# A state-space block with its FFN on one core: the first transposing load moves to ScalarE's queue, two evictions move to VectorE, and the written-out order changes

## The chip, the core and the metric

The kernel runs on one core of a Trainium2 chip. That core has a matrix engine (TensorE, PE in the profile; its weight loads are PEld), three engines for element-wise work (VectorE or DVE, ScalarE or ACT, GpSimd or POOL), and SyncE (SP), which here only issues DMAs. TensorE writes its results to PSUM, from where ScalarE or VectorE must copy ("evict") them to SBUF. DMAs are issued on the queue of an engine, SyncE's or ScalarE's, and the transfers of both are carried out by the core's 16 DMA engines. The metric is the device time of one execution in microseconds, as the median of several runs; lower is better.

## The reference

Inputs: q, k, v and the output are 2048 x 640 in bf16 (sequence by channels). Cut to what matters:

```python
k_shift = sum over t of 4 taps: k delayed by t * shift_k[:, t]     # short causal filter per channel
kv = k_shift * v
y  = causal convolution of kv with ssm_k along the sequence (by FFT in the reference) + kv * ssm_D
h  = x + layernorm(x) * y                                          # x is q
h2 = h + (silu(layernorm(h) @ w_gate) * (layernorm(h) @ w_up)) @ w_down
```

w_gate and w_up are 640 x 1728, w_down is 1728 x 640.

## The kernel before, in words

The sequence is cut into four blocks (0 to 3) of 512. The long convolution is done by blocks: each block of kv and each of the four blocks of the filter ssm_k is turned into a 512-point spectrum by matmuls with cosine and sine tables (`ftab`), spectra are multiplied and added on VectorE, and matmuls with `itab` turn them back.

The work of the front, before the first FFN, is:
- **Filter blocks 0 to 3.** `kload` (L527) loads block m of ssm_k into the tile kc; `ktrans` (L530) transposes it on TensorE in two groups of ten 128x128 transposes (L538), and ScalarE evicts each group to KT (L543). `kfwd` turns KT into spectra by `halves` (L573): matmuls L582, eviction L595 into C, R1 and KO, then butterflies on VectorE (L552). For block 0, VectorE also adds ssm_D to one row of KT (L547, "D", task 34) before the matmuls of kf0 may start.
- **kv.** `kv` (L671) loads k of the block transposed (channels on partitions) into kT with a transposing DMA (`tload`, L481, issued at L484) and v into vt. TensorE applies the four taps in three matmul groups (L691 for channels 0 to 511, L686 for the rest); ScalarE evicts them (block 0: L698; others: L715). In block 0 TensorE transposes the result back (L706) and VectorE multiplies it with v (L711); in the others transposing DMAs (kvo<-kT) do that and VectorE multiplies at L724. kT shares its memory with IO, an input of the inverse transform, so k of block i+1 can be loaded only when TensorE has read IO of block i.
- **The spectrum of kv** (`xfwd`: L582, evicted at L595 into X and FO), products (L753 to L769), the **inverse** (`inverse`, L817: matmuls L830, evicted at L845 by VectorE in block 0 and at L854 by ScalarE in blocks 1 to 3), the second layernorm, and a transposing DMA of the result into hnT (hnT<-qo). The FFN (L911, L912, L922, then the down-projection L954, L966) follows on hnT.

TensorE starts with 24 matmuls on zeros (L511, "spin"), which compute nothing. ScalarE's first ACTIVATE is a dummy Silu (L516), with the load of the function table in front of it.

**What sets the order.** Every operation is a numbered task, in the order in which the code adds them. `ORDER` (L307) is a table written out by hand or by a search outside of the kernel: for each of the five engines' queues the numbers of its tasks in the order in which they are issued. `schedule` walks it to assign PSUM tiles (four of two banks each), and `emit` puts semaphore waits in front of each task and writes the queues. A queue is worked off in its order: a task that waits holds back all behind it. The costs in the code serve that walk alone (PSUM tiles, and where `schedule` puts filler matmuls, L249, into a gap of TensorE that it foresees).

Task numbers that matter here: 0 identity matrix; 1 and 2 wcol and drow (the taps and ssm_D, on ScalarE's queue); 3 ftab; 13 spin; 14 Silu; 15 and 16 the tap matrices dg and dl on VectorE; 17, 57, 62, 67 the loads of filter blocks 0 to 3; 18 the transposing load of k, block 0; 19 v; 138 x, block 0. 20, 24 and 28 are the matmul groups of kv0, 21, 25 and 29 their evictions. 32 and 35 are the two groups of transposes of filter block 0, 33 and 36 their evictions. 37 to 52 are kf0 (odd: matmuls, even: evictions). 139 to 151 are the bn_stats of x. 192 to 195 are the inverse of block 0; 202, 209, 216, 223 its hnT transposes. 312, 313, 314 are x, k and v of block 1; 315, 319, 323 the matmul groups of kv1, 316, 320, 324 their evictions. 802 to 805 are the inverse of block 3 and 806, 815, 824, 833 its evictions.

Before the change tasks 18, 33 and 806 stand on the queues of SyncE, ScalarE and ScalarE.

Of the kernel before, what the change touches and what calls it, by code (L numbers as in the profile page):

```python
# [23 lines left out]
class _Task:  # L24
    __slots__ = ("eng", "fn", "cost", "lat", "deps", "after", "succ", "npred", "ready", "end", "start",
                 "opens", "tiles", "idx", "clock", "sem", "seq", "dma", "name", "gap", "lock", "fill", "late", "pause")
# [32 lines left out]
class _Graph:  # L59
# [38 lines left out]
    def add(self, eng, name, fn, cost, r=(), w=(), pr=(), pw=(), skip=(), lat=None, dma=None, after=(), lock=None):  # L98
# [9 lines left out]
        t.fill = 0  # L108
        t.pause = None
# [120 lines left out]
    def emit(self, block):  # L230
# [84 lines left out]
    """,  # L315
    "act": """
# [12 lines left out]
    """,  # L329
    "dve": """  # L330
# [10 lines left out]
    """,  # L341
    "pool": """
        5 10 6 8 7 9 11 153 197 218 204 200 211 221 207 214 338 423 405 396 414 531 626 608 599 617 734 838 820 829 811
    """,
    "sp": """
# [3 lines left out]
    """,  # L349
}  # L350


def bass_sequential_preLN__ssm_conv_h3__swiglu_ffn__prompt_kernel(
    nc: bass.Bass,
# [713 lines left out]
```

## Time and profile before

| | |
|---|---|
| median of 3 runs | 273.35 us (273.2 to 273.37) |
| profiled execution: first to last instruction (span) | 269.5 us |
| PE busy | 255.2 us (95%) |
| ScalarE busy | 206.9 us (77%) |
| VectorE busy | 203.8 us (76%) |
| DMA moved | 25.85 MB, 96 GB/s on the mean |
| granted TensorE clock | 0.998 |

The profile is one execution on the chip. Its times count from the first instruction; what lies outside of the span (the program's start and end) isn't in it. L12 is line 12 of the kernel before. A row such as `ACT L543 ACTIVATE KT<-ps 128x1280 x2 | idle` names the engine, the line, the operation, what it writes and reads, and how many of them are taken together; a bracket at the end gives the idle time of the engine before it and what ended it. SPq and ACTq are the queues' own instructions, such as the issuing of a DMA. The chain of waits follows the work that ended last back in time: each step goes to what released it. In the list of stretches each engine has its busy time; a row of DMA issues gives the bytes and the time from issue to landing; the rows "q8 instruction" and "q14 instruction" are the fetches of the engines' own program, in count, MB and share.

### The profile page before, as it was taken

To read this page: it belongs to the slowest core of one execution; us is meant where nothing else is said; L and a number is where in the kernel's file an instruction comes from. 1 tells how busy PE (TensorE), PEld (TensorE's weight loads), DVE (VectorE), ACT (ScalarE), POOL (GpSimd) and SP (SyncE) were. 2 spreads that over 40 slices of the span, in tenths; PEclk is the share of its full clock that TensorE was granted. 3 is DMA by queue.
4 is the path that set the end of the run, shared out by engine and by line. 5 is a ranking of instruction groups with operands and counts; after the bars stand their busy time and mean duration, and the time that the engine had idled before them with its cause. 6 is when DMAs were issued, how large, how long until landed. Compare 5 with 4: busy or idle time off the path is not lost.

```text
span 269.5 us, 4198 instructions
## 1 busy us (share of the span) xinstructions
PE 255.2 (95%) x1643; PEld 144.2 (53%) x1660; DVE 203.8 (76%) x282; ACT 206.9 (77%) x394; POOL 24.1 (9%) x35
## 2 busy tenths in 40 slices
PE   7799797999999999999999997999999999999995
PEld 5576455545444666554446574454446674444663
DVE  2399999899999999999999998999996100042312
ACT  2799999797889999479969997399889963647400
POOL 0000315000030013000200141000200200000000
PEclk9999999999999999999999999999999999999999
DMA  6999909551173608643000336510000050010002
GB/s 124 373 355 369 340 19 124 112 138 73 30 261 122 103 0 103 135 155 100 0 1 16 86 63 119 129 80 1 2 0 0 2 122 0 2 49 0 0 27 99
DMA packets 42501, 25.85 MB, mean 96 GB/s; under 512 B 32241, under 2 KB 41202, under 8 KB 42482
## 3 DMA queue, kind: packets, MB, share of 16 engines
q1 hardware_dynamic: 41824, 25.58, 35.7%
q8 instruction: 13, 0.21, 0.3%
q10 hardware_dynamic: 658, 0.01, 0.1%
q14 instruction: 6, 0.05, 0.1%
HBM read 15.69 MB, written 2.62 MB: 68 GB/s over the span
## 4 chain that ended last, share of the span: by engine, by line
DVE 41%; PE 27%; ACT 19%; DMA 6%; SPq 3%; issue 2%; POOL 1%; DVEq 0%
PE ps L954 11%; DVE T L753 6%; DVE T L754 6%; PE ps L912 6%; PE ps L911 5%; DVE T L759 5%; DVE Y L769 5%; DVE gu L938 4%; DVE X L552 3%; SPq L484 3%; DMA kT<-in_A_k_dram 3%; ACT KT L543 3%; ACT KO L595 2%; DVE C L666 2%; DMA kc<-in_A_ssm_k_dram 2%
## 5 line engine op out<-in xcount | busy, mean ns | idle before, releaser
L954 PE MATMUL ps<-Wd,gu 128*128 128x384 bf16 (+1 forms) x416 | 59.0, 299 | 0.2 <-ACT qo L854 0.2
L912 PE MATMUL ps<-hnT,UA 128*128 128x512 bf16 x140 | 53.1, 379 | 0.5
L911 PE MATMUL ps<-hnT,GA 128*128 128x512 bf16 x132 | 50.0, 379 | 1.3 <-DMA hnT<-qo 1.3
L954 PEld LDWEIGHTS ps<-Wd,gu 128*128 128x128 bf16 x416 | 40.0, 98 | 18.3 <-issue 1.3
L936 ACT ACTIVATE ub<-ps 128x512 bf16<-128x512 f32 (+1 forms) x60 | 33.7, 568 | 18.5 <-PE ps L912 11.3
L912 PE MATMUL ps<-hnT,UB 128*128 128x512 bf16 x120 | 45.5, 379 | 0.2
L911 PE MATMUL ps<-hnT,GB 128*128 128x512 bf16 x117 | 44.3, 379 | 0.0
L938 DVE TENSOR_TENSOR gu<-gu,ub 128x512 bf16<-128x512 bf16 x52 | 21.5, 421 | 25.1 <-ACT ub L936 13.2
L934 ACT ACTIVATE gu<-ps 128x512 bf16<-128x512 f32 x52 | 29.8, 596 | 12.6 <-PE ps L912 12.4
L753 DVE TENSOR_TENSOR T<-X,C 128x2560 bf16<-128x2560 bf16 x20 | 29.7, 1486 | 0.2
L754 DVE TENSOR_TENSOR T<-X,C 128x2560 bf16<-128x2560 bf16 x20 | 29.7, 1486 | 0.1
L911 PEld LDWEIGHTS ps<-hnT,GA 128*128 128x128 bf16 x140 | 13.7, 98 | 18.2 <-DMA hnT<-qo 1.9
L582 PE MATMUL ps<-KT,ftab 128*128 128x320 bf16 x128 | 19.9, 300 | 2.5 <-ACT KT L543 1.8
L912 PEld LDWEIGHTS ps<-hnT,UA 128*128 128x128 bf16 x140 | 13.7, 98 | 15.7
L881 POOL TENSOR_TENSOR mv<-mv,half 128x1 f32<-128x1 f32 x16 | 13.7, 859 | 68.2 <-ACT mv L874 68.2
L911 PEld LDWEIGHTS ps<-hnT,GB 128*128 128x128 bf16 x120 | 11.7, 98 | 14.2 <-ACT ub L936 0.2
L759 DVE TENSOR_TENSOR T<-T 128x1280 bf16<-128x1280 bf16 x24 | 19.2, 819 | 0.1
L912 PEld LDWEIGHTS ps<-hnT,UB 128*128 128x128 bf16 x120 | 11.7, 98 | 14.0
L582 PE MATMUL ps<-vt,ftab 128*128 128x320 bf16 x128 | 19.0, 299 | 0.1
L804 POOL TENSOR_TENSOR st<-st,half 128x8 f32<-128x8 f32 x4 | 7.9, 1981 | 113.1 <-ACT st L798 113.1
L769 DVE TENSOR_TENSOR Y<-Y,T 128x2560 bf16<-128x2560 bf16 x12 | 17.8, 1484 | 0.0
L582 PEld LDWEIGHTS ps<-KT,ftab 128*128 128x128 bf16 x128 | 11.0, 98 | 10.7 <-ACT KT L543 3.1
(86 smaller groups left out, 376.5 us busy)
## 6 DMA issues: line engine op xcount, KB each, us to landing
kc<-in_A_ssm_k_dram SPq DMA_DIRECT2D x4, 640.0 KB, 10.1
vt<-in_A_v_dram SPq DMA_DIRECT2D x4, 640.0 KB, 4.8
xh<-in_A_q_dram SPq DMA_DIRECT2D x4, 640.0 KB, 5.9
out_dram<-xh SPq DMA_DIRECT2D x16, 160.0 KB, 2.0
Wd<-in_B_w_down_dram SPq DMA_DIRECT2D x1, 1280.0 KB, 7.5
UA<-in_B_w_up_dram SPq DMA_DIRECT2D x1, 1120.0 KB, 13.5
GA<-in_B_w_gate_dram SPq DMA_DIRECT2D x1, 1120.0 KB, 10.5
UB<-in_B_w_up_dram SPq DMA_DIRECT2D x1, 960.0 KB, 7.5
```

The lines of the kernel that those rows point to most:

```text
L582: last = e.matmul(pt.f(c, W), ftab[:, cs, j, f * P:(f + 1) * P], src[:, j, c * W:(c + 1) * W], start=(j == par), stop=(j == par + 2))
L753: g.add("dve", nm, lambda e, x=x, k=k, t1=t1: e.tensor_tensor(out=t1, in0=x, in1=k, op=ALU.mult), cdve(2560), r=[x, k], w=[t1])
L754: g.add("dve", nm, lambda e, x=x, k=ksw, t2=t2: e.tensor_tensor(out=t2, in0=x, in1=k, op=ALU.mult), cdve(2560), r=[x, k], w=[t2])
L759: g.add("dve", nm, lambda e, p=p, q=q, d=d, op=op: e.tensor_tensor(out=d, in0=p, in1=q, op=op), cdve(1280), r=[p, q], w=[d])
L769: g.add("dve", nm, lambda e, y=y, z=z: e.tensor_tensor(out=y, in0=y, in1=z, op=ALU.add), cdve(2560), r=[y, z], w=[y])
L881: g.add("pool", nm, lambda e, m=m: e.tensor_tensor(out=m[:, 3:4], in0=m[:, 2:3], in1=half[:, 1, 0:1], op=ALU.pow), 650, r=[m[:, 2:3], half ...
L911: e.matmul(pt.f(0, N), wg[:, c, f0:f0 + P], hnT[:, c, :], start=(c == 0), stop=(c == NC5 - 1))
L912: last = e.matmul(pt.f(1, N), wu[:, c, f0:f0 + P], hnT[:, c, :], start=(c == 0), stop=(c == NC5 - 1))
L934: g.add("act", nm, lambda e, pt=pt, gv=gv, a=ps_g, ts=ts: e.activation(out=gv, in_=pt.f(a[0], N, a[1])[:, ts], func=ACTF.Silu, scale=gain) ...
L936: g.add("act", nm, lambda e, pt=pt, uv=uv, a=ps_u, ts=ts: e.activation(out=uv, in_=pt.f(a[0], N, a[1])[:, ts], func=ACTF.Copy, scale=gain) ...
L938: g.add("dve", nm, lambda e, uv=uv, gv=gv: e.tensor_tensor(out=gv, in0=gv, in1=uv, op=ALU.mult), cdve(n), r=[gv, uv], w=[gv])
L954: last = e.matmul(pt.flat(c1 - c0, P + c0), slots[fb][:, j * P:(j + 1) * P], Wd[:, fb, c0:c1], start=(fb == 0 and not second), stop=(fb == ...
```

## The change

There are three edits.
1. `tload` takes the queue as an argument, and for block 0 the transposing load of k (task 18) is issued on ScalarE's queue.
2. A new helper `evict` makes the PSUM evictions that were written out before. For the numbers in `VECTOR` (33 and 806) it makes them on VectorE as tensor_copy or tensor_scalar; for all others the same ACTIVATE as before.
3. `ORDER` has new lists for all five queues.

The code (the unchanged lines around and the other callers of `evict` are left out):

```diff
+VECTOR = """
+    33 806
+"""
...
+        def evict(name, out, src, n, w, pr, scale=1.0, bias=None, r=(), after=()):
+            if len(g.tasks) in on_vector:
+                if bias is None and scale == 1.0:
+                    fn = lambda e: e.tensor_copy(out=out, in_=src())
+                elif bias is None:
+                    fn = lambda e: e.tensor_scalar(out=out, in0=src(), scalar1=scale, scalar2=None, op0=ALU.mult)
+                elif scale == 1.0:
+                    fn = lambda e: e.tensor_scalar(out=out, in0=src(), scalar1=bias, scalar2=None, op0=ALU.add)
+                else:
+                    fn = lambda e: e.tensor_scalar(out=out, in0=src(), scalar1=scale, scalar2=bias, op0=ALU.mult, op1=ALU.add)
+                t = g.add("dve", name, fn, cps(n), r=r, w=w, pr=pr)
+            else:
+                kw = {"func": ACTF.Copy} if bias is None else {"func": ACTF.Identity, "bias": bias}
+                t = g.add("act", name, lambda e: e.activation(out=out, in_=src(), scale=scale, **kw), cact(n, bias is not None),
+                          r=r, w=w, pr=pr, after=after)
...
-        def tload(name, dst, src, rows, cols, lat, **kw):
+        def tload(name, dst, src, rows, cols, lat, eng="sp", **kw):
             n = rows * cols // 2048
             pipe = 18.5 * n
+            if eng != "sp":
+                return g.add(eng, name, lambda e: e.dma_start_transpose(dst, src), 3450, w=[dst], dma=(1900, 1900), lat=lat, lock=False, **kw)
...
-                g.add("act", "kt%d" % m, lambda e, pt=pt, dst=dst: e.activation(out=dst, in_=pt.h2(D), func=ACTF.Copy), cact(1280),
-                      w=[dst], pr=[pt], after=first_act)
+                evict("kt%d" % m, dst, pt_view(pt, lambda p: p.h2(D)), 1280, [dst], [pt], after=first_act)
...
-                tload("kT0", kT[:, :, 16:N + 16], K2[0:N, :], N, D, 2400)
+                tload("kT0", kT[:, :, 16:N + 16], K2[0:N, :], N, D, 2400, eng="act")
...
-                    g.add("act", nm, lambda e, pt=pt, q2=q2, s=s, j=j: e.activation(out=q2, in_=pt.f2(W), func=ACTF.Identity, bias=s[:, 3, j:j + 1],
-                                                                                     scale=-1.0 if i > 1 else 1.0),
-                          cact(D, 1), r=[s[:, 3, j:j + 1]], w=[q[:]], pr=[pt])
+                    evict(nm, q2, pt_view(pt, lambda p: p.f2(W)), D, [q[:]], [pt], scale=-1.0 if i > 1 else 1.0, bias=s[:, 3, j:j + 1],
+                          r=[s[:, 3, j:j + 1]])
```

The heads of the order lists, as far as block 1's kv (the lists go on, changed, to the end):

```diff
 pe
-13 20 24 32 22 35 26 28 39 47 43 37 41 30 51 45 49 170 162 164 166 160 60 172 58 168 174 82 72 80 65 70 63 86 74 68 78 120
-118 84 124 116 114 128 76 192 193 195 194 126 108 96 319 122 104 315 323 94 102 98 100 106 238 234 ...
+13 32 35 20 28 24 22 45 39 51 26 30 43 41 37 160 164 162 166 49 60 170 47 168 172 86 174 78 58 70 63 65 94 118 80 84
+74 72 82 68 76 195 194 193 192 124 104 122 100 98 319 96 323 116 108 106 102 126 315 128 120 234 238 ...
 act
-1 14 2 21 25 33 36 29 40 48 44 38 42 52 46 50 171 163 165 167 161 61 59 169 175 173 73 81 83 152 71 64 87 66 79 69 75 121 ...
+1 2 18 14 36 21 29 25 46 40 52 44 42 38 161 165 163 167 50 61 48 152 169 171 173 87 175 59 71 64 66 79 95 119 159 81 ...
 dve
-12 15 16 23 34 27 139 140 141 142 31 143 53 144 145 55 146 54 147 56 148 176 149 177 150 180 181 151 178 183 182 179 185 ...
+12 15 16 33 139 34 140 141 142 143 144 145 23 27 31 146 147 148 149 53 150 54 176 177 151 180 181 55 56 178 183 154 ...
 sp
-0 18 17 19 3 138 4 57 225 228 67 62 312 314 232 227 229 224 233 313 202 223 209 216 322 ...
+17 0 138 3 19 57 224 228 4 62 67 232 227 229 226 225 313 216 223 209 202 312 325 314 ...
```

In the new lists 806 stands last of the four evictions of block 3's inverse.

More of the change, by code (lines that the diff above doesn't have):

```diff
@@ L25 @@
     __slots__ = ("eng", "fn", "cost", "lat", "deps", "after", "succ", "npred", "ready", "end", "start",
-                 "opens", "tiles", "idx", "clock", "sem", "seq", "dma", "name", "gap", "lock", "fill", "late", "pause")
+                 "opens", "tiles", "idx", "clock", "sem", "seq", "dma", "name", "gap", "lock", "fill", "late", "pause", "alt")
 class _Tile:
@@ L108, in add @@
         t.fill = 0
+        t.alt = None
         t.pause = None
@@ L308 @@
     "pe": """
[6 rows of a table removed]
[7 rows of a table added]
     """,
     "act": """
[12 rows of a table removed]
[12 rows of a table added]
     """,
     "dve": """
[10 rows of a table removed]
[10 rows of a table added]
     """,
     "pool": """
-        5 10 6 8 7 9 11 153 197 218 204 200 211 221 207 214 338 423 405 396 414 531 626 608 599 617 734 838 820 829 811
+        10 11 5 6 8 7 9 153 218 211 204 221 214 197 207 200 338 423 414 405 396 531 626 608 617 599 734 838 829 820 811
     """,
     "sp": """
[3 rows of a table removed]
-    """,
-}
[3 rows of a table added]
+    """,
+}
+VECTOR = """
+    33 806
+"""
 def bass_sequential_preLN__ssm_conv_h3__swiglu_ffn__prompt_kernel(
@@ L476, in cps, with pt_view @@
             return (n + 65) / 0.96
+        on_vector = {int(x) for x in VECTOR.split()}
+        def pt_view(pt, f):
+            return lambda: f(pt)
+        def evict(name, out, src, n, w, pr, scale=1.0, bias=None, r=(), after=()):
[13 more added lines that the diff above has]
+                          r=r, w=w, pr=pr, after=after)
+            a = (("act", cact(n, bias is not None)), ("dve", cps(n)))[t.eng == "act"]
+            t.alt = (*a, LATENCY[a[0]])
+            return t
         def load(name, dst, src, nbytes, eng="sp", late=0, **kw):
             return g.add(eng, name, lambda e: e.dma_start(dst, src), 450, w=[dst], dma=(nbytes / 345.0, 0), lat=1700 + late, **kw)
-        def tload(name, dst, src, rows, cols, lat, **kw):
+        def tload(name, dst, src, rows, cols, lat, eng="sp", **kw):
             n = rows * cols // 2048
             pipe = 18.5 * n
+            if eng != "sp":
+                return g.add(eng, name, lambda e: e.dma_start_transpose(dst, src), 3450, w=[dst], dma=(1900, 1900), lat=lat, lock=False, **kw)
             return g.add("sp", name, lambda e: e.dma_start_transpose(dst, src), 830 + 12.8 * n, r=kw.pop("r", ()), w=[dst],
@@ L569, in eighths @@
                     d = dst[:, f, pl, :]
-                    g.add("act", name, lambda e, pt=pt, d=d, sg=sg: e.activation(out=d.rearrange("p (b x) -> p b x", b=2), in_=pt.f2(W),
-                                                                         func=ACTF.Copy, scale=sg * scale), cact(D), w=[d], pr=[pt])
+                    evict(name, d.rearrange("p (b x) -> p b x", b=2), pt_view(pt, lambda p: p.f2(W)), D, [d], [pt], scale=sg * scale)
         def halves(cls, name, src, ev, od, scale, m, direct=False):
@@ L594, in halves @@
                         d = (od if par else ev)[:, f, pl, :]
-                        g.add("act", name, lambda e, pt=pt, d=d, sg=sg: e.activation(out=d.rearrange("p (b x) -> p b x", b=2), in_=pt.f2(W),
-                                                                             func=ACTF.Copy, scale=sg * scale), cact(D), w=[d], pr=[pt])
+                        evict(name, d.rearrange("p (b x) -> p b x", b=2), pt_view(pt, lambda p: p.f2(W)), D, [d], [pt], scale=sg * scale)
         def kfwd(m, dst):
@@ L625, in quarters @@
                     d = od[:, r // 2, pl, :] if r % 2 else ev[:, r, pl, :]
-                    g.add("act", name, lambda e, pt=pt, d=d, sg=sg: e.activation(out=d.rearrange("p (b x) -> p b x", b=2), in_=pt.f2(W),
-                                                                         func=ACTF.Copy, scale=sg * scale), cact(D), w=[d], pr=[pt])
+                    evict(name, d.rearrange("p (b x) -> p b x", b=2), pt_view(pt, lambda p: p.f2(W)), D, [d], [pt], scale=sg * scale)
         def tt2(name, op, out, a_, b_):
@@ L697, in kv @@
                 if i in PT:
-                    g.add("act", nm, lambda e, pt=pt, ks=ks, nb=nb: e.activation(out=ks, in_=pt.f2(N)[:, 0:nb], func=ACTF.Copy),
-                          cact(N * nb), w=[ks], pr=[pt])
+                    evict(nm, ks, pt_view(pt, lambda p, nb=nb: p.f2(N)[:, 0:nb]), N * nb, [ks], [pt])
                     tp = g.tile("kt")
@@ L714, in kv @@
                     continue
-                g.add("act", nm, lambda e, pt=pt, ks=ks, nb=nb: e.activation(
-                    out=ks.rearrange("p b (j x) -> p b j x", j=4), in_=pt.f2(N)[:, 0:nb].rearrange("p b (x j) -> p b j x", j=4),
-                    func=ACTF.Copy), cact(N * nb), w=[ks], pr=[pt])
+                evict(nm, ks.rearrange("p b (j x) -> p b j x", j=4),
+                      pt_view(pt, lambda p, nb=nb: p.f2(N)[:, 0:nb].rearrange("p b (x j) -> p b j x", j=4)), N * nb, [ks], [pt])
                 for h in range(nb):
```

61 rows, old and new, of the table ORDER are left out of this document.

## The prediction

> **What bounds the kernel now.** I read the page first, then the busy time of the engines by stretch, then the chain of waits in order of time, then the timeline of each engine over the first 50 us.
>
> ```profile
> span 269.5 us, 4198 instructions
> ```
>
> The median of the runs is 273.35 us, so 3.85 us lie outside the span; I leave them as they are and work on the span. The stretches give, after the length, the busy time of PE, PEld, DVE, ACT and POOL.
>
> ```profile
> 13.78:47.77 33.99, 29.25 (x248) 19.32 (x250) 32.87 (x55) 33.96 (x56) 6.53 (x9) 1.00 0.83 237
> 47.67:140.00 92.33, 91.75 (x553) 48.88 (x562) 90.20 (x113) 78.87 (x156) 7.37 (x6) 1.00 0.39 97
> 140.00:170.00 30.00, 27.76 (x204) 16.71 (x205) 28.07 (x38) 25.81 (x52) 5.56 (x4) 1.00 0.34 72
> ```
>
> From 13.78 to 47.77 ScalarE is full (33.96 of 33.99 us); from 47.67 on TensorE is (91.75 of 92.33), with VectorE almost as full beside it. TensorE's work there is fixed, so the end is its start into that stage plus its idle time in it, and of that the stretch 140 to 170 holds the part worth naming (2.24 us). What sets the start is in the chain of waits:
>
> ```profile
> 1.14 3.46 SPq L484
> 4.66 4.84 DMA kc<-in_A_ssm_k_dram
> 9.55 0.75 PE ps L538 x10
> ...
> 13.78 1.30 ACT C L595 x2
> ...
> 40.61 7.02 DMA kT<-in_A_k_dram
> 47.67 1.06 PE ps L691 x16
> ```
>
> SyncE's queue spends 3.46 us on issuing the transposing load of k (L484); only then does it issue the first load of the filter (kc), which is there 4.84 us later, and the path goes on through TensorE's transposes of kc to ScalarE's first eviction of C at 13.78. So the 3.46 us stand on the path that sets the end.
>
> **Part 1: the load moves to ScalarE's queue.** The rows that carry the front are ScalarE's, then TensorE's, then the k load's own time from issue to landing:
>
> ```profile
> 0.72 0.46 ACTq L479 DMA_DIRECT2D wcol<-in_A_shift_k_dram  x1
> 1.21 1.28 ACT L516 ACT_TABLE_LOAD   x1 [1.21 <-PEq L1053]
> 1.28 0.56 ACTq L479 DMA_DIRECT2D drow<-in_A_ssm_D_dram  x1
> 2.50 0.20 ACT L516 ACTIVATE qo<-gz 128x2 bf16<-128x2 bf16 x1
> 7.78 1.94 ACT L698 ACTIVATE kT<-ps 128x1024 bf16<-128x1024 f32 x2 [5.07 <-PE ps L691]
> 10.33 2.37 ACT L543 ACTIVATE KT<-ps 128x1280 bf16<-128x1280 bf16 x2 [0.61 <-PE ps L538]
> 12.70 0.60 ACT L698 ACTIVATE kT<-ps 128x512 bf16<-128x512 f32 x1
> ```
>
> ```profile
> 1.04 5.10 PE L511 MATMUL ps<-gz 128*128 128x256 bf16 x24 [1.04 <-DVE gz L506]
> 6.67 1.92 PE L691 MATMUL ps<-kT,dg 64*64 64x512 bf16 x32 [0.53 <-DMA kT<-in_A_k_dram]
> ```
>
> ```profile
> 11.85 0.81 PE L686 MATMUL ps<-kT,dl 128*128 128x512 bf16 x3
> ```
>
> ```profile
> kT<-in_A_k_dram SPq DMA_TRANSPOSE x1, 5.5
> ```
>
> On SyncE kc is now first: issued at 0.72 instead of 4.66, landing at 0.72 + 4.84 = 5.6. TensorE spins on zeros until 6.14, then does the two groups of kc transposes, some 0.6 us each, done by 7.3 (before: from 9.55 on). On ScalarE's queue the k load follows wcol and drow, so it starts at 1.9. Its issue takes the same 3.46 us, to 5.36, and it lands 5.5 us after its start, at 7.4 (before: where TensorE starts on it, 6.67). Behind it on ScalarE wait the table load (1.28) and the dummy Silu (0.20), now done at 6.84. The 5.07 us that ScalarE sat idle hide them; its first real work comes at 7.4.
>
> From there TensorE does kv0 as tasks 20, 28, 24, from 7.4 to 10.1 (half of 1.92, 0.81, half of 1.92). ScalarE evicts task 36 from 7.4 to 8.55 (half of 2.37, less the overlap), then 21 and 29 to 10.1 (0.95 and 0.60) and 25, which waits for TensorE, to 11.1. That is what it had done by 13.78 before, but for task 33, which is VectorE's now. **Gain: 13.78 - 11.1 = 2.65 us.** After that ScalarE is full for 34 us as before, so the gain is kept as long as its inputs come as much earlier. The loads do:
>
> ```profile
> DMA packets 8029, 7.53 MB, mean 318 GB/s; under 512 B 4199, under 2 KB 7400, under 8 KB 8028
> ```
>
> ```profile
> DMA packets 4626, 6.81 MB, mean 356 GB/s; under 512 B 809, under 2 KB 3997, under 8 KB 4625
> ```
>
> The first row is 1.5 to 25.2 us, the second 6.1 to 25.2, after the k load. At the second's rate the 7.53 MB of the first take 21.2 instead of 23.7 us, so the last filter blocks come 2.5 us earlier: the gain of ScalarE within 0.2.
>
> The unknown is what k's transposing load suffers with another queue's loads beside it: here it ran alone, and the trace has no such pair. At least nothing (lands 7.4; I see nothing that would make it faster). At most it waits for all that is queued up to filter block 1 (by the code 3.2 MB, 9.0 us at 356 GB/s): 0.72 + 9.0 + 5.5, landing at 15.2. Each us after 7.4 costs one, since tasks 20, 28 and 24 stand ahead of kf0 on TensorE. The nearest rows are transposing loads that met a little foreign traffic, two instruction fetches between 44.0 and 47.6 us; then the hnT loads issued in that time, the hnT loads of the whole span, and k's loads of blocks 1, 2 and 3:
>
> ```profile
> q8 instruction: 1, 0.02, 1.9%
> q14 instruction: 1, 0.01, 0.7%
> ```
>
> ```profile
> hnT<-qo SPq DMA_TRANSPOSE x2, 3.6
> ```
>
> ```profile
> hnT<-qo SPq DMA_TRANSPOSE x16, 2.6
> ```
>
> ```profile
> kT<-in_A_k_dram SPq DMA_TRANSPOSE x1, 7.0
> ```
>
> ```profile
> kT<-in_A_k_dram SPq DMA_TRANSPOSE x1, 5.2
> ```
>
> ```profile
> kT<-in_A_k_dram SPq DMA_TRANSPOSE x1, 4.8
> ```
>
> Block 1's load, with the two fetches in its way, took 7.0 us where its sisters took 5.2 and 4.8: about 1 us for each fetch. So foreign packets do hold transposes up. But a fetch is one packet of 0.01 or 0.02 MB, a load's are all under 8 KB, and the k load is paced by its own 3.46 us of issue, which leaves turns to others. I take 0.4 us, near the undisturbed rows. **Part 1: -2.65 + 0.4 = -2.25 us.**
>
> The Trainium skill says (DMA: Bandwidth & Descriptors, Issuing engines are not separate DMA queues) that loads issued by different engines run on the same 16 DMA engines and interleave, and that a second issuer saves only issue time. That speaks against the change, but by the chain above issue time is just what is paid here.
>
> **Part 2: two evictions move to VectorE.** No row shows a plain copy out of PSUM on VectorE. The nearest (busy, mean ns) from below, for the smaller tile, and from above:
>
> ```profile
> L552 DVE TENSOR_TENSOR X<-X,FO 128x1280 bf16<-128x1280 bf16 x16 | 13.0, 818 | 0.1
> ```
>
> ```profile
> L845 DVE SCALAR_TENSOR_TENSOR xh<-ps,st,xh 128x640 bf16<-128x640 f32 x4 | 3.4, 878 | 0.1
> ```
>
> ```profile
> L711 DVE TENSOR_TENSOR vt<-ps,vt 128x1024 bf16<-128x1024 f32 x2 | 2.5, 1225 | 6.8 <-PE ps L538 6.8
> ```
>
> Task 33 (1280 elements) lies between 0.82 and 1.5 us (1.225 x 1.25); I take 1.4, near the row that reads PSUM. It runs from about 6.9 to 8.3, inside the 6.8 us in which VectorE stood idle until 11.36, so it costs nothing; its worth, 1.13 us off ScalarE, is counted above. Queued behind it are the first bn_stats and then task 34, for which kf0 waits (TensorE is there at 10.4). bn_stats wants x, now third on SyncE, as v was before:
>
> ```profile
> vt<-in_A_v_dram SPq DMA_DIRECT2D x1, 640.0 KB, 6.0
> ```
>
> Issued at 1.7, x lands at 7.7, or 8.5 with the k load beside it. If it came after 10, kf0 would slip as much. VectorE's dense stretch then starts at about 8.5 instead of 11.36, so VectorE doesn't take the 2.65 back.
>
> Task 806 (640 elements, scale and bias) takes some 0.88 there and about as long on ScalarE: nothing either way, at the end of VectorE's dense stretch, with TensorE's down-projection of block 2 beside it. If that cover were gone it would cost the 0.1 to 0.3 by which VectorE may be late for it.
>
> **Part 3: the order.** Every queue is reordered. On SyncE k's load of block 1 (task 313) goes ahead of x and v of block 1, which come after the four hnT transposes now. It follows the inverse, as before, so it is issued about 2.65 earlier, at 38.0, and lands between 43.2 (5.2 us) and 45.0 (7.0 us). ScalarE gets to kv1's evictions at 47.77 - 2.65 - 0.6 = 44.5 (five instead of six evictions of kf stand ahead in its new list), but one more kf group (0.6) is left to do after them: the two cancel, and the fetch delay in block 1 is hidden or costs 0.5. I take 0. After that the order can win or lose at places like these:
>
> ```profile
> 162.86 0.81 PE L686 MATMUL ps<-kT,dl 128*128 128x512 bf16 x3 [0.61 <-ACT kT L715]
> ```
>
> ```profile
> 168.53 0.39 PE L911 MATMUL ps<-hnT,GA 128*128 128x512 bf16 x1 [1.33 <-DMA hnT<-qo]
> ```
>
> They are 1.94 of the 2.24 us, one of them a late hnT transpose. At best both go; at worst other transposes meet fetches and as much is added. Between +1.9 and -1.9 I take 0.
>
> Sum: -2.65 + 0.4 + 0 + 0 = -2.25; 273.35 - 2.25 = **271.1 us**.
>
> **Rivals.**
>
> (a) The k load is held up by the loads beside it: slower. If it gets every second turn, its 3.46 us become 6.9 and it lands at 10.9; kv0 and its evictions are done at 14.6 instead of 13.78: 273.35 + 0.8 = 274.2. From a landing at 10.1 on the kernel is slower; 15.2 gives 278.5. For it: block 1's 7.0 us. Against: issue paces the load. Chance 0.25.
>
> The alternation is what the Trainium skill (DMA: Bandwidth & Descriptors, Queues, rings and completion order) states: each DMA engine takes turns between queues, packet by packet. The trace shows no two load queues at work together.
>
> (b) The front gains 2.25, and the new order gives 1.7 to 2.8 back in waits after 47: TensorE and VectorE are both full there, so a wait on either is paid. 272.8 to 273.9, within 0.2% (0.55 us), about what a measurement of this kernel can tell from no change. Chance 0.12.
>
> (c) The front gains 2.25 and the stalls at 162 and 168 go too: 271.1 - 1.9 = 269.2. Chance 0.15.
>
> The forecast, 269.8 to 272.8, has 0.48. Faster 0.48 + 0.15 = 0.63; same 0.12; slower 0.25. The range takes in (c) with 0.4 us to spare and (a) up to a landing at 11.2, 268.8 to 274.5; beyond it lie a fifth of (c) and two thirds of (a).
>
> **What would show it.** Right: kc's transposes on TensorE directly behind the spin, at 6.2; kv0 at 7.4 to 8.0; ScalarE dense from about 11; k's block 1 issued at about 38; kv1 on TensorE at about 44.5. Wrong by (a): TensorE waits for kT beyond 9 and ScalarE is idle until after 12. Wrong by (b): TensorE's idle time after kv1 is over 5 us. If x lands after 10, VectorE's first bn_stats waits for it and kf0 is late.

## The result, and the profile after

| | before | after |
|---|---|---|
| median of 4 runs each | 273.27 us (272.43 to 273.37) | 292.06 us (290.7 to 292.89) |
| ratio, 95% interval | | 1.0694 (1.065 to 1.0737) |
| profiled execution's span | 269.5 us | 290.0 us |

The change makes the kernel 6.9% slower. The forecast was 271.1 us, faster; it went the way of rival (a), k held up by the loads beside it, but far beyond the 278.5 us that the prediction gave as that rival's worst.

The page of the kernel after: its span, the clock that was granted in 40 slices, and the packets, MB and share of the second DMA queue (q10, the one that ScalarE issues on).

```profile
span 290.0 us, 4189 instructions
...
PEclk9655999999999999999999999999999999999999
...
q10 hardware_dynamic: 3250, 0.66, 2.0%
```

The same row of the page before:

```profile
q10 hardware_dynamic: 658, 0.01, 0.1%
```

So the k load is 3250 - 658 = 2592 packets and 0.65 MB: some 250 bytes a packet. The span grew by 20.5 us, and the stretches show where (length, then the busy time of PE, PEld, DVE, ACT and POOL, the clock, the DMA engines' share and GB/s):

```profile
6.20:26.04 19.84, 1.31 (x21) 1.16 (x22) 5.84 (x11) 2.61 (x3) 0.00 (x0) 0.58 1.14 239
26.04:34.00 7.96, 7.96 (x72) 4.08 (x73) 1.75 (x2) 4.54 (x6) 0.00 (x0) 0.76 0.49 154
26.04:63.49 37.45, 33.73 (x283) 20.67 (x283) 30.32 (x46) 33.73 (x55) 5.99 (x8) 0.95 0.48 137
```

For 19.84 us no engine has much work (TensorE 1.31 us, VectorE 5.84, ScalarE 2.61), while the DMA engines are full (share 1.14; the times of packets are added up and can overlap). kv1, the first matmul group on k of block 1, starts at 63.49 where it started at 47.67: 15.8 of the 20.5 us. The other 4.7 come behind it: 226.5 us from there to the end of the span, in place of 221.8. The chain of waits says what the first 26 us are:

```profile
1.99 24.01 DMA kT<-in_A_k_dram
26.04 1.92 PE ps L719 x9
...
57.83 5.61 DMA kT<-in_A_k_dram
63.49 1.06 PE ps L719 x16
```

One DMA, the load that was moved: 24.01 us in place of 5.5. ScalarE's and then TensorE's timeline:

```profile
1.99 13.49 ACTq L515 DMA_TRANSPOSE kT<-in_A_k_dram  x1
15.51 1.28 ACT L548 ACT_TABLE_LOAD   x1 [15.51 <-issue]
16.80 0.20 ACT L548 ACTIVATE qo<-gz 128x2 bf16<-128x2 bf16 x1
16.91 1.22 ACT L502 ACTIVATE KT<-ps 128x1280 bf16<-128x1280 bf16 x1
```

```profile
6.68 1.31 PE L570 MATMUL ps<-ident,kc 128*128 128x128 bf16 x20 [0.48 <-DMA ident<-cst_id]
26.04 1.92 PE L719 MATMUL ps<-kT,dg 64*64 64x512 bf16 x16 [18.05 <-DMA kT<-in_A_k_dram]
```

The instruction that issues the load holds ScalarE's queue for 13.49 us (3.46 on SyncE before), and the table load and all evictions stand behind it; TensorE does the transposes of kc half a us later than forecast (6.68, held by the identity matrix), and then waits 18.05 us for k. VectorE makes its eviction (task 33, L492) and has little else to do:

```profile
8.40 0.82 DVE L492 COPY KT<-ps 128x1280 bf16<-128x1280 bf16 x1
```

The DMA packets of both load queues say why. First from 3.4 to 25.9 us, then from 8 to 20 us (packets, MB, share of the 16 engines; q1 is SyncE's queue):

```profile
q1 hardware_dynamic: 3242, 4.83, 86.4%
q10 hardware_dynamic: 3229, 0.66, 25.7%
```

```profile
q1 hardware_dynamic: 1426, 2.54, 81.6%
q10 hardware_dynamic: 1433, 0.37, 24.8%
```

While both queues have packets, they go one for one: 1426 to 1433. (The first row of q10 holds some 640 packets of the small loads too; those of k come from 6.4 us on.) k's 2592 packets are 162 turns on each of the 16 engines. Within the 19.6 us from 6.4 to 26.0 a turn takes 121 ns on the mean: k's packet of 250 bytes and one of SyncE's, 1.5 KB on the mean (4.83 MB / 3242). Alone, a packet of k takes at most 30 ns (4.83 us / 162, from the first run below). SyncE's queue is never empty in that time, since the loads behind filter block 1 keep coming. The Trainium skill (DMA: Bandwidth & Descriptors, Queues, rings and completion order) has the engines take turns between queues by whole packets; the equal counts agree. The turns don't hold all of the delay: k's first packet comes 4.4 us after the issue began, where k alone needed 1.4 (3.2 to 3.4 us is the first stretch with one). What holds the first packet up stays open.

### The profile page after: what moved, and what is told of

Read it like the earlier page. It is cut to its first block, busy times and chain, and to the rows that moved or that the text cites. A ratio compares the mean times of both kernels' runs of the same rounds, so it can differ in the third digit from the quotient of the medians.

```text
span 290.0 us, 4189 instructions
## 1 busy us (share of the span) xinstructions
PE 258.8 (89%) x1650; PEld 143.2 (49%) x1650; DVE 205.7 (71%) x284; ACT 204.3 (70%) x392; POOL 26.6 (9%) x35
## 3 DMA queue, kind: packets, MB, share of 16 engines
q10 hardware_dynamic: 3250, 0.66, 2.0%
## 4 chain that ended last, share of the span: by engine, by line
PE 41%; ACT 23%; DVE 15%; DMA 13%; SPq 2%; POOL 2%; issue 2%; ACTq 0%; DVEq 0%
PE ps L936 12%; PE ps L937 12%; DMA kT<-in_A_k_dram 10%; PE ps L979 9%; PE ps L612 3%; ACT xh L839 3%; ACT qo L893 3%; ACT qo L502 3%; DVE T L780 2%; ACT ub L961 2%; ACT qo L895 2%; DVE X L583 2%; SPq L516 2%; ACT qo L911 2%; DVE C L583 2%; DVE T L779 2%
## 5 line engine op out<-in xcount | busy, mean ns | idle before, releaser
L936 PE MATMUL ps<-hnT,GA 128*128 128x512 bf16 x140 | 53.1, 379 | 2.1 <-DMA hnT<-qo 2.1
L936 PE MATMUL ps<-hnT,GB 128*128 128x512 bf16 x120 | 45.5, 379 | 0.0
L719 PE MATMUL ps<-kT,dg 64*64 64x512 bf16 x128 | 9.2, 414 | 19.3 <-DMA kT<-in_A_k_dram 19.1
L906 POOL TENSOR_TENSOR mv<-mv,half 128x1 f32<-128x1 f32 x16 | 17.0, 1068 | 61.5 <-ACT mv L899 61.5
L502 ACT ACTIVATE kT<-ps 128x1024 bf16<-128x1024 f32 (+1 forms) x12 | 10.5, 884 | 11.3 <-PE ps L719 10.3
```

The lines of the kernel that those rows point to most:

```text
L502: t = g.add("act", name, lambda e: e.activation(out=out, in_=src(), scale=scale, **kw), cact(n, bias is not None), r=r, w=w, pr=pr, after= ...
L906: g.add("pool", nm, lambda e, m=m: e.tensor_tensor(out=m[:, 3:4], in0=m[:, 2:3], in1=half[:, 1, 0:1], op=ALU.pow), 650, r=[m[:, 2:3], half ...
L936: e.matmul(pt.f(0, N), wg[:, c, f0:f0 + P], hnT[:, c, :], start=(c == 0), stop=(c == NC5 - 1))
```

## The experiments

Three theories were set against each other first. **S**: k's load shares the DMA engines with SyncE's loads, turn by turn. **Q**: ScalarE's own queue is slow for such a load, whatever is beside it. **O**: the loss is the new order's or the moved evictions'. All runs keep the whole computation. The kernel before had medians of 272.64, 272.37, 270.98 (one run) and 272.26 us beside them, in the order of the groups below.

### Group 1: sharing, the queue or the order

**k alone on ScalarE's queue.** The changed kernel; all of SyncE's loads but the identity matrix wait for k:

```diff
-        17 0 138 3 19 57 ...
+        0 17 138 3 19 57 ...
+        for n in (17, 138,):
+            g.tasks[n].deps.add(g.tasks[18])
```

> The changed kernel, but filter block 0 and every load behind it on SyncE's queue wait until the k load has landed; only the identity matrix and the two small loads are beside it. Theory S (sharing: the k load is held up by SyncE's loads, because the DMA engines take turns between the two queues packet by packet): its issue is back at about 3.5 us and it lands 5.5 us after its start, at about 7.5; the kernel is then some 275 to 279, since the other loads start 6 us late. Rival Q (a transposing load is slow when ScalarE's queue issues it): issue 13.5 us and landing 24 us after its start as in the changed kernel, and over 292 us in all.

Measured: 279.26 us (one run), just above the 279 that S gave at most. The load's issue on ScalarE, and its row in the chain:

```profile
1.87 2.84 ACTq L515 DMA_TRANSPOSE kT<-in_A_k_dram  x1
```

```profile
1.87 4.83 DMA kT<-in_A_k_dram
```

Issue 2.84 us, landed after 4.83: Q falls, and the 13.49 us of issue come from the loads beside it, not from that queue. What is left to lose here is kc, which waits for k and lands at 11.58.

**Only part 1, on the kernel before**: k on ScalarE's queue, in the old order and without moved evictions.

```diff
-                tload("kT0", kT[:, :, 16:N + 16], K2[0:N, :], N, D, 2400)
+                tload("kT0", kT[:, :, 16:N + 16], K2[0:N, :], N, D, 2400, eng="act")
 act
-        1 14 2 21 25 33 36 ...
+        1 2 18 14 21 25 33 36 ...
 sp
-        0 18 17 19 3 138 ...
+        0 17 19 3 138 ...
```

> The kernel before, with nothing changed but the k load's queue (ScalarE's, behind the two small loads). S and Q: the k load lands at about 26 as in the changed kernel, and the time is 273.3 plus about 19, some 290 to 293. Rival O (the loss comes from the new order and the evictions, and the late k load is hidden in the old order): under 280.

Measured: 291.66 us (one run). TensorE's wait:

```profile
25.58 3.63 PE L693 MATMUL ps<-kT,dg 64*64 64x512 bf16 x32 [19.73 <-DMA kT<-in_A_k_dram]
```

The whole loss comes from this one edit: O falls as its cause. The packets go one for one here too, 1358 to 1362 from 8 to 20 us. But the way to the same time is another. kv1 starts at 67.26, 3.8 us later than in the changed kernel, and 222.3 us from there end the span, in place of 226.5. 2.1 of the 3.8 us are there when k of block 1 is issued (59.92, in the changed kernel 57.83), the other 1.7 are that load's own time (7.3 in place of 5.6).

**k on SyncE's queue, first.** The changed kernel with the load in its old place, ahead of kc (18 leaves ScalarE's list as well).

```diff
-                tload(..., N, D, 2400, eng="act")
+                tload(..., N, D, 2400)
 sp
-        17 0 138 3 19 57 ...
+        0 18 17 138 3 19 57 ...
```

> The changed kernel with the k load back on SyncE's queue, behind the identity matrix and ahead of everything, as before; the two evictions on VectorE and the new order stay. S and Q: the whole loss is gone, 271 to 275 (filter block 0 lands at 9.5 as before, and TensorE's new order does its transposes ahead of kv0, which costs up to 2 us; ScalarE has 1.13 us less). O: over 280.

Measured: 277.02 us, ratio 1.0144 (1.0102 to 1.0186). O is out again, but S's 271 to 275 is missed as well. k landed at 6.54, kc at 9.47, and TensorE, whose new order wants kc first, waited 3.76 us for it, where up to 2 were expected.

**kc, then k, on SyncE's queue**, the rest as in the run above.

```diff
-        17 0 138 3 19 57 ...
+        17 0 18 138 3 19 57 ...
```

> As the one before, but on SyncE's one queue filter block 0 comes first, then the identity matrix, then the k load, then the rest: the landing order that the prediction counted on, without a second queue. If the prediction's sum for the front is right where nothing shares the transfer, filter block 0 lands at about 5 and k at about 8, ScalarE is dense from about 11.5, and the time is 270.5 to 272.5. If the gain of the front is given back further on (rival b), 272.8 to 274.

Measured: 274.19 us, ratio 1.0062 (1.003 to 1.0094). k landed at 8.22, and kv1 started here:

```profile
44.70 1.06 PE L719 MATMUL ps<-kT,dg 64*64 64x512 bf16 x16 [0.81 <-DMA kT<-in_A_k_dram]
```

That is 3.0 us earlier than before, and within 0.2 us of the 44.5 that the prediction gave for an undisturbed k. Yet the kernel is slower than before: rival (b), in a size that the prediction did not allow. And the agreement at kv1 is half chance. kv1 waits for the load of k of block 1, here as in the kernel before:

```profile
39.22 5.44 DMA kT<-in_A_k_dram
```

Before, it was issued at 40.61 and took 7.02 us. So the front is 1.4 us earlier, where the prediction had the issue at 38.0, 2.65 earlier; the other 1.6 us are the load's own time. One instruction fetch falls into it here, and two did before:

```profile
q14 instruction: 1, 0.01, 1.3%
```

Nor is the work ahead of it the same. Ahead of that issue ScalarE has 14 evictions of KO and C in place of 17 before, and ahead of kv1 9 of KO in place of 13. They are not saved: they follow behind it. (What the 1.4 us come from, the earlier front or the three evictions, is not separated by this run.) Matmuls of the filter are put off behind kv1's start too, first before, then here:

```profile
L582 PE MATMUL ps<-KT,ftab 128*128 128x320 bf16 x28 | 4.1, 299 | 0.0
```

```profile
L612 PE MATMUL ps<-KT,ftab 128*128 128x320 bf16 x36 | 5.6, 300 | 0.0
```

That gives back 1.5 us where TensorE is full. Another part is this wait:

```profile
113.26 0.38 PE L937 MATMUL ps<-hnT,UA 128*128 128x512 bf16 x1 [2.70 <-DMA hnT<-qo]
```

### Group 2: evictions and order

**Task 33 alone on VectorE**, in the kernel before.

```diff
+VECTOR = "33"
 act
-        1 14 2 21 25 33 36 29 40 ...
+        1 14 2 21 25 36 29 40 ...
 dve
-        12 15 16 23 34 27 139 ...
+        12 15 16 33 23 34 27 139 ...
```

> The kernel before with one edit: task 33, the first eviction of filter block 0, goes to VectorE (in front of the product with v and of D). Loads and order as before. ScalarE has 1.13 us less to do in the stretch where it is full, and VectorE is idle there: the sum of the prediction has 1.13 us for this alone. VectorE's product with v waits for a later task, so task 33 in front of it costs nothing. Theory: 272.1 to 272.6 us where before has 273.3 (ratio 0.996). Rival: what ScalarE gains is lost in later waits: within 0.2 % of before.

Measured: 273.27 us, ratio 1.0006 (0.9974 to 1.0038): nothing, the rival. The chain of waits up to ScalarE's first C:

```profile
5.24 6.03 DMA vt<-in_A_v_dram
11.36 1.24 DVE vt L737
12.62 0.49 DVE KT L577
13.15 0.73 PE ps L611 x4
13.91 1.30 ACT C L501 x2
```

C (13.91, before 13.78) needs the matmuls of kf0, and these need D (task 34, L577), which stands on VectorE behind the product with v; v landed at 11.27. In the kernel before the product starts at the same 11.36. So what ScalarE no longer does it spends waiting.

**kc first, old order, evictions as before.**

```diff
 pe
-        13 20 24 32 22 35 26 28 39 ...
+        13 32 35 20 24 28 22 26 39 ...
 act
-        1 14 2 21 25 33 36 29 40 ...
+        1 14 2 33 36 21 25 29 40 ...
 sp
-        0 18 17 19 3 138 ...
+        17 0 18 19 3 138 ...
```

> The kernel before with filter block 0 in front of k on SyncE's queue and the tasks of filter block 0 in front of those of kv0 on TensorE and ScalarE; all the rest of the old order is kept (no eviction on VectorE, x still behind v and the table). It tells the front from the new order behind it. kc lands at 5.6, k at 8.2 (as in the run with kc and then k on SyncE's queue, where kv1 started 3.0 us earlier than before and 5 us were given back after it). Theory F (the give-back belongs to the new order): ScalarE is dense from about 8 us with the same work, so it gains up to 2 us, and with the old order behind it idle time of TensorE after kv1 stays at 3.3 to 4 us: 271.0 to 272.3. Rival G (whatever starts kv1 earlier loses it again, since TensorE then meets late loads): 273 to 274.5.

Measured: 272.03 us, ratio 0.9968 (0.9939 to 0.9996), inside F's range, but not for F's reason: there was no gain in the front to keep.

```profile
14.16 1.30 ACT L595 ACTIVATE C<-ps 128x640 bf16<-128x640 f32 x2 [2.26 <-PE ps L582]
```

C comes at 14.16, later than before, since D (at 12.88) still stands behind the product with v. k of block 1 is issued at 40.99, 0.4 us later than before; kv1 starts at 47.40 all the same, because that load takes 6.4 us in place of 7.0, and 222.0 us follow. It is the one kernel of the study whose interval lies below the kernel before, by 0.3%, and barely.

**The same with task 33 on VectorE.**

```diff
+VECTOR = "33"
 act
-        1 14 2 33 36 21 25 29 40 ...
+        1 14 2 36 21 25 29 40 ...
 dve
-        12 15 16 23 34 27 139 ...
+        12 15 16 33 34 23 27 139 ...
```

> The kernel before with filter block 0 in front of k on SyncE's queue (and in front of kv0 on TensorE and ScalarE), and with task 33 on VectorE as well; the rest of the old order is kept. Theory F (the give-back after kv1 belongs to the new order): 0.5 to 1.1 us less than with task 33 on ScalarE: 270.0 to 271.5, faster than both kernels. Rival G (whatever starts kv1 earlier loses it again): 273 to 274.5, like the run with kc and then k on SyncE's queue and the new order.

Measured: 272.14 us, ratio 0.9982 (0.9951 to 1.0013). k of block 1 was issued at 40.56 and kv1 started at 47.78, both about as before, though C came at 13.35: the chain runs through the load of the last filter blocks, which landed at 26.04. Neither F's 270.0 to 271.5 nor G's 273 to 274.5.

**kc, then k, with x and v of block 1 early.** The last run of group 1, with one edit of SyncE's list:

```diff
-        ... 313 216 223 209 202 312 325 314 321 318 ...
+        ... 312 314 313 216 223 209 202 325 321 318 ...
```

> The run with kc and then k on SyncE's queue and the new order (274.19, idle time of TensorE after kv1 6.43 us, of it 2.70 on one hnT transpose at 113), with one edit: x and v of block 1 go ahead of k of block 1 and of the hnT transposes again, as before the change. If the late x and v of block 1 push the transposing loads of the FFN (hnT, kvo) together, the 2.70 us wait goes: 271.5 to 272.5. Rival: the wait comes from the order on TensorE and VectorE and stays: 273.5 to 275.

Measured: 272.86 us, ratio 1.0012 (0.9977 to 1.0047); 1.3 us less than without the edit, by the medians (the two intervals overlap). The wait for hnT shrinks, and the four loads of hnT in front of it are issued in 5.53 us in place of 6.47. SyncE's queue without and with the edit, then TensorE with it:

```profile
105.16 6.47 SPq L516 DMA_TRANSPOSE hnT<-qo  x4
```

```profile
104.52 5.53 SPq L516 DMA_TRANSPOSE hnT<-qo  x4
```

```profile
111.46 0.39 PE L936 MATMUL ps<-hnT,GA 128*128 128x512 bf16 x1 [1.54 <-DMA hnT<-qo]
```

The time lies between the two ranges. The wait did not go, as the first theory had it, but became 1.2 us shorter; its remainder is of the size of the 1.33 us of the kernel before.

### Group 3: how the sharing works, and what the clock adds

**Only kc beside k**: the changed kernel, with x and all behind it on SyncE made to wait for k.

```diff
+        for n in (138,):
+            g.tasks[n].deps.add(g.tasks[18])
```

> The changed kernel, but on SyncE's queue only filter block 0 (kc) and the identity matrix go beside k's load; x and all loads behind it wait until k has landed. Theory S (turns, packet by packet): kc has some 40 packets of 1 KB for each DMA engine, at 64 to 94 ns each (estimate from the times of the loads in the changed kernel's trace), against k's 160 packets of 256 B that take 4.8 us alone; so k is delayed by at most 2.6 to 3.8 us and lands at 7.5 to 10 (alone 6.7, beside everything 26.0), and kc lands at 6 to 6.5. Theory B (k simply waits until all that is queued on SyncE has gone): 0.66 MB at 356 GB/s, 1.8 us, lands at 8.5: no difference to S here. Theory Q (the load is slow on ScalarE's queue whatever is beside it) is already ruled out. x lands late, at about 12 to 13, so VectorE and kf0 wait some 2 to 3 us: 274 to 277 us in all.

Measured: 277.49 us (one run), just above the 277 expected. The chain's row, and the packets from 3.4 to 8.1 us:

```profile
1.99 6.17 DMA kT<-in_A_k_dram
```

```profile
q10 hardware_dynamic: 3197, 0.66, 73.0%
q1 hardware_dynamic: 525, 0.42, 26.9%
```

One load of 0.65 MB beside it, and k lands 6.17 us after its start in place of 4.83. The delay of 1.34 us goes with the 0.42 MB of q1 that were served in that time (3.2 us for a MB); in the changed kernel 24.01 - 4.83 = 19.2 us go with 4.83 MB (4.0 us for a MB). So the price goes with what gets its turns before k is done, and a single load cannot take many. x landed at 11.89 in this run, so nothing is won.

**The four filter loads first beside k**, in the changed kernel.

```diff
-        17 0 138 3 19 57 224 228 4 62 67 232 ...
+        17 0 57 62 67 138 3 19 224 228 4 232 ...
```

> The changed kernel with the four filter loads (packets of 1 KB) first on SyncE's queue, and x, the table and v (larger packets) behind them. The bytes on SyncE's queue are the same. Theory S: each of k's 160 turns per DMA engine now stands against a packet of 1 KB, 30 + 64 to 94 ns a pair, so k lands at 15 to 20 us after its start, at 17 to 22, clearly ahead of the 26.0 of the changed kernel, and its issue takes 8 to 11 us in place of 13.49. Theory B (k waits for the bytes queued beside it): the same bytes, so it lands at 26 or later. x comes late, so the whole is no guide: 285 to 295 us.

Measured: 293.18 us (one run). The chain's row, and the packets from 8.4 to 12 and from 12 to 16 us:

```profile
1.99 20.11 DMA kT<-in_A_k_dram
```

```profile
q1 hardware_dynamic: 1026, 1.04, 81.4%
q10 hardware_dynamic: 1029, 0.26, 32.2%
```

```profile
q1 hardware_dynamic: 374, 1.37, 95.4%
q10 hardware_dynamic: 370, 0.09, 10.7%
```

k landed at 22.1, just outside S's range and well ahead of the 26 of B; the issue took 7.95 us, at S's lower end. B's premise, the same bytes ahead of k, isn't borne out: from 3.4 to 22 us 5.53 MB went by, in less time than 4.83 MB did. S shows within this one run: the packets go one for one in both stretches, and a turn takes 56 ns (3.6 us x 16 / 1029) beside packets of 1.0 KB and 173 ns (4 us x 16 / 370) beside packets of 3.7 KB. Size is not all of it: from 8 to 20 us a turn took 94 ns beside packets of 1.8 KB on the mean, in the changed kernel 134 ns beside packets of the same mean; what else lengthens a turn stays open. From 8 to 20 us the counts are 2048 to 2045; over all of k's time SyncE's are more, since k's first packet comes only at 6.4 us and its packets thin out at the end (213 to 851 from 20 to 22 us).

**TensorE kept busy while it waits**: 190 filler matmuls in front of task 20. (They multiply the identity matrix, not zeros as the expectation says; the result isn't used.)

```diff
+                    if t.seq == 20:
+                        t.fill = 190
```

> The changed kernel with 190 matmuls on zeros in front of kv0's first group, so that TensorE has work while it waits for k and its clock needn't drop. k still lands at 25 to 26. If the clock that was granted after the wait (0.58, then 0.76 until 34 us) costs time of its own, kv0's groups take 1.06 and 0.8 us again and the whole is 1 to 2 us faster than the changed kernel: 289 to 291 us where that had 291 to 292. If ScalarE sets the pace there anyway, the time stays within 0.5 us of the changed kernel's.

Measured: 287.84 us (one run), less than the 289 to 291 expected. The stretch from k's landing to kv1, and the first group of kv0:

```profile
23.61:59.45 35.84, 31.97 (x282) 20.36 (x282) 30.43 (x46) 33.79 (x55) 5.97 (x8) 1.00 0.50 141
```

```profile
23.61 1.06 PE L721 MATMUL ps<-kT,dg 64*64 64x512 bf16 x16 [0.34 <-DMA kT<-in_A_k_dram]
```

35.84 us in place of 37.45, at a clock of 1.00 in place of 0.95: the clock that dropped in the wait costs 1.6 us of its own (one run each). The rest of what this run is faster comes from k, which landed 2.4 us earlier (23.57 in place of 25.99) with the same loads beside it. The turns are one for one here too (1872 to 1882 from 8 to 20 us) but shorter, 102 ns in place of 134, beside packets of 1.5 KB on the mean in place of 1.8; why the landing moves from run to run stays open.

### Group 4: a last attempt at the front

**kc first and kf0 early, old order behind.**

```diff
 pe
-        13 20 24 32 22 35 26 28 39 47 43 37 41 ...
+        13 32 35 20 28 39 24 47 22 43 26 37 41 ...
 act
-        1 14 2 21 25 33 36 29 40 ...
+        1 14 2 33 36 21 29 40 25 ...
 dve
-        12 15 16 23 34 27 139 ...
+        12 15 16 34 23 27 139 ...
 sp
-        0 18 17 19 3 138 4 57 225 228 67 62 312 ...
+        17 0 18 3 19 138 57 67 62 4 225 228 312 ...
```

> The kernel before with filter block 0 in front of k on SyncE's queue, as in the run with kc first and the old order, and with what held that run up put right: there ScalarE was done with its first five evictions at 11.9 but had to wait until 14.16 for kf0, since on TensorE the transposes back of kv0 and on VectorE the product with v stood in front of kf0. Here the first two groups of kf0 go directly behind the groups of kv0 that they need not wait for, D goes in front of the product with v, and the loads of filter blocks 1 to 3 go in front of the FFN weights, because block 3 landed at about 25.9 in every order. All behind that is the old order. Theory F (a gain in the front is kept when the order behind it is the old one): ScalarE is full from 7 us on, so its stretch ends up to 1.9 us earlier (7.05 + 4.8 + 33.99 = 45.84 in place of 47.77), and with 218.6 to 218.8 us from kv1 to TensorE's end as in the old order: 270.4 to 271.8 us where before has 272.4 to 273.3, ratio 0.994 to 0.997. Rival G (what is gained in the front is lost behind it, in waits for transposing loads): ratio 0.998 to 1.005.

Measured: 272.49 us, ratio 1.0015 (0.9983 to 1.0047): no gain, in G's range but not for G's reason, since 221.5 us from kv1 to the end are no more than before. ScalarE's first C came at 11.10 in place of 13.78, and yet kv1 started at 48.44, later than before. The chain of waits of this run, and the stretch from VectorE's first product with v up to kv1, first of the kernel before, then of this one:

```profile
13.19 1.24 DVE vt L711
...
27.94 0.30 ACT st L798
...
41.34 7.05 DMA kT<-in_A_k_dram
```

```profile
11.36:47.67 36.31, 31.10 (x258) 20.33 (x257) 35.15 (x57) 35.79 (x59) 6.53 (x9) 1.00 0.85 250
```

```profile
13.16:48.44 35.28, 29.93 (x255) 19.88 (x254) 34.43 (x56) 33.80 (x55) 6.33 (x9) 1.00 0.81 233
```

VectorE is the third busy time: 35.15 of 36.31 us and 34.43 of 35.28. It is as full as ScalarE, and here it began 1.8 us later, on the product with v, which waited 4.54 us for TensorE. From 13.19 to 27.92 the chain runs through VectorE alone; then it goes over to ScalarE (27.94, before 27.48), whose evictions lead to the issue of k of block 1 at 41.34 in place of 40.61. By this chain ScalarE's lead of 2.7 us at C was lost in what VectorE had to deliver. A version in which both begin early was not tried.

## Why the prediction was wrong, point by point

**The step that failed is the sharing in part 1**: "I take 0.4 us", with a landing at 7.4 and at most at 15.2. k landed at 25.99, so the term is 18.6 us. The runs with k alone (4.83 us from start to landing) and with part 1 alone (the whole loss) show that this is the cause; the equal counts and the two turn lengths in one run (56 and 173 ns) show that it is turns. Three things went wrong in it.
- "The k load is paced by its own 3.46 us of issue, which leaves turns to others": issue doesn't pace the load; issue itself grew with what the DMA engines had to do. It took 2.84 us with free engines and 13.49 with full ones.
- Rival (a) let every second turn double the time, as if a foreign packet were as long as one of k's. The row of packets under 512 B had the answer: k is some 2600 packets of about 250 B, 162 turns an engine, and at most 30 ns alone become 121 ns beside packets of 1.5 KB.
- The upper bound counted what was queued up to filter block 1. SyncE goes on issuing, so the turns go on until k is done; the bound had to be k's turns times a turn's length, not the bytes queued at its start.

**The gain in the front, 2.65 us**, was not reached. With k on SyncE behind kc, kv1 did start at 44.70 against the forecast 44.5, but that was in part luck: k of block 1 was issued 1.4 us earlier, not 2.65, and the rest is that load's shorter time, which the prediction had let cancel. Evictions and matmuls had also been put off behind kv1. x landed at 10.3 in that run, and D waited behind the first bn_stats, as the prediction had warned; C came at 12.64, not at 11.1. Where the same work stands ahead as before (kc first in the old order, with or without task 33 on VectorE, and kf0 early), k of block 1 was issued at 40.99, 40.56 and 41.34, against 40.61: no gain. The prediction took the path from kc to C as the one that sets the start. The chains show others beside it: v's load, the product with v and D, and VectorE, which is as full as ScalarE. The step "one more kf group (0.6) is left to do" is mis-sized: eight matmuls more, two groups, 1.5 us of TensorE.

**Task 33** took 0.82 us on VectorE, the lower bound, where 1.4 was taken, and it was hidden, as said. But the 1.13 us off ScalarE were worth nothing alone, since C waits for D, and D for v and the product with it. **Task 806** took 0.884 us, as said.

**Part 3**, 0 within 1.9 either way: the new order costs 4.7 us behind kv1 in the changed kernel, 5.1 with k behind kc on SyncE. Of the latter some 1.3 go with the late x and v of block 1 and 1.5 are the filter's matmuls put off; the remaining 2 or so were not taken apart.

**The time outside of the span** isn't 3.85 us: the profiled execution after took 292.19 us, 2.2 more than its span. 273.35 belonged to other executions than the 269.5; the run of the kernel before beside the last group that spanned 269.5 us took 271.44.

Right were the early transposes of kc (6.68, forecast 6.2; held by the identity matrix, which came at 6.63 behind kc) and the landing of an undisturbed k on ScalarE's queue (6.70, forecast 7.4). The Trainium skill's rule that a second issuer saves issue time only (DMA: Bandwidth & Descriptors, Issuing engines are not separate DMA queues) was set aside, because issue time was what seemed to be paid. The trace goes beyond the rule: the second issuer cost 19 us.

## What to carry to other kernels

A load of many small packets on a queue of its own, beside a queue full of large ones, was served a packet a turn here: before moving one, count its packets for each DMA engine and multiply by the length of a turn (in one run 56 ns beside packets of 1.0 KB and 173 beside 3.7 KB), for as long as the other queue stays filled. A transposing load whose result is needed early cost less in the others' queue than beside it (274.19 behind kc, 277.02 ahead of it, 292.06 beside). And where two engines are equally full in a stretch, an earlier start of one was worth nothing while the other started late; a later stage that begins earlier may only have had work put behind it, or a load that happened to be shorter.

## What the runs showed of the hardware

- A DMA's issue takes longer when the DMA engines have more to do, and the queue of the engine that issues it stands still meanwhile: 2.84 us alone, 4.18 beside one load, 7.95, 12.51, 13.49 and 14.66 beside many, for the same transposing load.
- Two load queues were served packet for packet while both had packets: 1426 to 1433, 1358 to 1362, 1872 to 1882 and 2048 to 2045 in four kernels from 8 to 20 us. The length of a turn went with the size of the other packet, 56 ns at 1.0 KB and 173 ns at 3.7 KB in one run.
- After 18 us without work TensorE was granted 0.76 of its clock for the next 8 us (0.58 in the wait). The first group of kv0 took 1.92 us in place of 1.06; 190 filler matmuls in the wait brought it back to 1.06.
- A copy of 128 x 1280 bf16 values out of PSUM took VectorE 0.82 us, no more than an addition of that size in SBUF, where a product out of PSUM with 128 x 1024 fp32 values takes 1.22.
